# Three edits in one kernel: where subtractions run, when four blocks are split, and how the last step's results are laid out and stored

## The chip, the cores and the metric

One core of one Trainium2 chip runs the whole program. The metric is the device time of one execution in microseconds (us). Three runs of the kernel before give the times shown below.

## The reference, cut to what matters

```python
# attention with keys and values pooled by 8 over the sequence: B=8, H=8, S=576, D=64
k_p = k.reshape(B, H, Sp, 8, D).mean(axis=3); v_p = v.reshape(B, H, Sp, 8, D).mean(axis=3)
attn = softmax(q @ k_p^T / sqrt(D)); x = (attn @ v_p) as 4608 tokens x 512
...
h = x @ w_in                       # first layer: 512 -> 2048
y = relu(h) ** 2 @ w_out           # 2048 -> 512
...
gate = sigmoid(y @ w_gate); val = y @ w_val      # second layer: 512 -> 1536, twice
out = (gate * val) @ w_out2                      # 1536 -> 512
```

## The kernel before, in words

Everything is kept with features on partitions and tokens along the free axis. A float32 number is split into a rounded part (hi) and a remainder (lo); a product is three TensorE passes over such pairs. hi is a copy on ScalarE, lo a subtraction on VectorE.

**First layer.** Nine blocks of 512 tokens. For each of 16 slices f of the hidden width: 12 matmuls into a bank `h` (line 801), relu on ScalarE (line 845), square on VectorE (line 851), hi on ScalarE (line 855), lo on VectorE (line 858), 12 matmuls into four banks `acc` (line 810). Two banks `h` and three tiles `g` are in turn; the second set of matmuls of f stands behind the first set of f + 2. Attention for later blocks runs between. The result y goes to DRAM (`y_dram`).

**Second layer.** Six blocks b of 768 tokens, and the 1536 hidden columns in three chunks c: 18 steps (c, b), with b running up, down and up again. Each step uses a seven-product scheme for 2 x 2 blocks of matrices. y is cut in quadrants B11, B12, B21, B22, and needs the differences T1 to T4; weights need S1 to S4. So the matmul operands are seven tiles for each of two halves k2, hi and lo: 14 tiles, in buffers listed in `y_tags` (eleven that the first layer's weights leave free at its end, and three of their own, `ys`). `y_prep` makes them in chunk 0: it loads y from DRAM (line 1015), forms four differences for each half on GpSimd (line 1068), hi on ScalarE (line 1047), lo on VectorE (line 1051), and stores all 14 to `ys_dram` (line 1054). In chunks 1 and 2 `y_load` loads them back (line 1095). The weights of a chunk are prepared by `w_prep` (sums on GpSimd, lines 1165 to 1177; lo on VectorE, line 1132).

A step has two groups fp of products (line 1220): 14 products each, added up on VectorE from the PSUM banks (line 1251), sigmoid on ScalarE, multiplied (line 1285). The product of gate and val is again cut in quadrants; four differences t1, t3, t2, t4 for each group run on GpSimd (line 1313), each waiting for the one before; hi and lo (lines 1301, 1305) give the seven tiles `p`. Then come the outputs (line 1350): M1, M2, M6, M5, M7, M3, M4, each for two 128-row halves a and b, added up on VectorE (line 1395). Chunks 0 and 1 store partial sums in DRAM (`o_part`); chunk 2 turns each result by 32 x 32 blocks on VectorE (line 1412) and stores `out` in rows of 128 numbers, 32 partitions to a DMA (line 1425), eight DMAs for a step.

**What sets the order.** All operations are given to a planner (`Plan`) with an engine, a duration and a rank. It plays them through in time and writes out one order for each engine: at each moment the ready operation of the lowest rank goes first. On the chip each engine follows its list strictly in order, so an operation that waits holds up all behind it. All DMAs are issued by SyncE (SP).

```python
self.op("pool", 1.0, fn, deps, t - 50)      # engine, planned time, what, after what, rank
...
(y_prep if nxt[0] == 0 else y_load)(nxt[1], t + BT, t)   # the next block, during this step
```

Of the kernel before, what the change touches and what calls it, by code (L numbers as in the profile page):

```python
# [134 lines left out]
def kernel(  # L135
# [12 lines left out]
    nc = tc.nc  # L148
# [818 lines left out]

    ORDER = ("M1", "M2", "M6", "M5", "M7", "M3", "M4")
    YO = ("B11", "B21", "T2", "T1", "T3", "B22", "T4")
    W = {"M1": ("A11", "B11", "X"), "M2": ("A12", "B21", "Y"), "M6": ("S2", "T2", "X"), "M5": ("S1", "T1", "Y"),  # L970
# [29 lines left out]

    def y_prep(b, rank, at):
        t0 = b * TN
        blks = {x for x in range(t0 // NA, -(-(t0 + TN) // NA))}
        y_deps = [o for x in blks for o in y_stored[x]] + [opened]
        for name in YO:
            ys_ready[name] = []
        for k2 in range(2):
            y_prep_half(b, rank, at, k2, t0, y_deps)

    def y_prep_half(b, rank, at, k2, t0, y_deps):  # L1010
        st = {}
# [29 lines left out]
        def split(name):  # L1041
            n = YO.index(name)
            x = y_tags[2 * n + k2]

# [13 lines left out]
            o = los[name] = op("dve", 0.6, lo, [o], r)  # L1058
            ys_ready[name].append(o)
            ys_stored[b, 2 * n + k2] = op("dma", 1.3, keep, [o], r + 30, lag=2.0)  # L1060

        made = {}

        def make(name, a, c, deps):
            def fn():
                if name == "T1":
                    st["yt"] = bp["r"].tile([128, HN], F32, tag="yt", name="yt", bufs=1)
                nc.gpsimd.tensor_tensor(out=q(name), in0=q(a), in1=q(c), op=ALU.subtract)

            made[name] = op("pool", 1.0, fn, deps, rank - 30 + 0.05 * k2, take=("yt",) if name == "T1" else ())  # L1070

# [133 lines left out]
    def products(c, b, fp, t):  # L1205
# [105 lines left out]
        def diff(dst, a, z, deps):  # L1311
            def fn():
                nc.gpsimd.tensor_tensor(  # L1313
                    out=st["gate", dst], in0=st["gate", a], in1=st["gate", z], op=ALU.subtract)

            return op("pool", 1.0, fn, deps, t - 50)

# [15 lines left out]
    def outputs(c, b, t):  # L1333
# [3 lines left out]
        o_tag = {0: "o", 1: ("o", "yf", "w2s")[c]}  # L1337
        t0 = b * TN

        def mm(a, m, k2, n, deps, take):  # L1340
# [3 lines left out]
            def fn():  # L1344
# [4 lines left out]
                for j, (wa, yc) in enumerate(PASSES):  # L1349
# [4 lines left out]

            o = op("pe", 3 * DP, fn, list(deps) + [wslot_ready[c, NFP, i], p_ready[y, k2]], t + D1 * n + 0.5 * D1 * k2,
                   take=(bank[z, a],) if take else ())
# [35 lines left out]
        def add(a, key, z, deps, give=()):  # L1392
            def fn():
                x = st[a, key]
                nc.vector.tensor_tensor(out=x, in0=x, in1=st[z, a][:, 0:HN], op=ALU.add)  # L1395

            return op("dve", 0.56, fn, deps, t - 50, give=give)

        def finish(a, key, o, n):
            tt = t + D1 * n  # L1400
            if not fin:
# [4 lines left out]
                return  # L1406
            u, h = a + 2 * (int(key[0]) - 1), int(key[1]) - 1

            def turn():
# [7 lines left out]
            if first:  # L1417
                t_own[h] = ("yf", P.last["yf"])
            turned[h].append(x)
            if len(turned[h]) < 4:  # L1420
                return
            r0 = t0 + h * HN

# [9 lines left out]
        C = {}  # L1433
        order = ["M1a", "M1b", "M2a", "M2b", "M6a", "M6b", "M5a", "M5b", "M7a", "M7b", "M3a", "M4a", "M4b", "M3b"]
        for n, x in enumerate(order):
# [29 lines left out]
    for fp in range(NFP):  # L1465
        w_prep(0, fp, tl + 4 + 14 * fp, tl)
    w_prep(0, NFP, tl + 34, tl)
    y_prep(0, TB, tl)
    for step, (c, b) in enumerate(steps):
        t = TB + BT * step  # L1470
        y_users.clear()
        p_users = defaultdict(list)
# [12 lines left out]
        elif nxt:  # L1485
            (y_prep if nxt[0] == 0 else y_load)(nxt[1], t + BT, t)

# [34 lines left out]
```

## Time and profile before

| what | value |
|---|---|
| median of three runs | 1732.56 us (1730.58 to 1734.37) |
| the profiled execution's own time | 1728.68 us |
| its span, first to last instruction | 1726.6 us |
| TensorE busy | 1697.7 us, 98% |
| VectorE busy | 1184.6 us, 69% |
| ScalarE busy | 800.8 us, 46% |
| GpSimd busy | 282.4 us, 16% |
| DMA, share of 16 engines' span | 47.7% |

The busy time of an engine is the sum of its instructions' durations. TensorE's matmuls overlap, so its share counts pauses of more than about 0.2 us only. The profiled execution lies 0.22% under the median of the runs.

### The profile page before, as it was taken

Reading aid. Unit: us, or ns where it says so; the run is one execution under the profiler, and the core shown is the slowest. Engines: PE = TensorE matmul, PEld = TensorE weight load, DVE = VectorE, ACT = ScalarE, POOL = GpSimd, SP = SyncE. Lnnn points to the kernel's source line nnn. Section 1 sums busy time; section 2 is a strip of 40 time slices with the busy share of each in tenths; the row PEclk is TensorE's granted clock in tenths of the full one; section 3 lists DMA queues with packets and bytes.
Section 4 is the critical chain, followed back from the end, with each engine's and each line's share of the span. In section 5 each row is a group of like instructions: output and inputs, shape, how many; then the busy total and the mean of one; then the engine's idle time right before and its main releaser. Section 6 shows DMA issues by size and latency. Waiting matters only on the chain.

```text
span 1726.6 us, 25822 instructions
## 1 busy us (share of the span) xinstructions
PE 1697.7 (98%) x9096; PEld 1513.5 (88%) x9096; DVE 1184.6 (69%) x2200; ACT 800.8 (46%) x1927; POOL 282.4 (16%) x270
## 2 busy tenths in 40 slices
PE   8999999999999999999999999999999999999997
PEld 5778878878888888878888999999999999999997
DVE  7898668878685865423458666778655568766665
ACT  6776644444443443322446555566333345333332
POOL 0000000000000000000224334445222215222222
PEclk9999999999999999999999999999999999999999
DMA  9732344455444433020226455535555563766662
GB/s 285 250 93 75 85 124 106 122 149 126 133 113 124 106 104 95 25 87 1 73 102 225 165 201 192 195 141 171 185 195 195 197 201 114 219 201 202 201 201 38
DMA packets 224162, 251.16 MB, mean 145 GB/s; under 512 B 75040, under 2 KB 165920, under 8 KB 224032
## 3 DMA queue, kind: packets, MB, share of 16 engines
q1 hardware_dynamic: 224032, 249.50, 47.7%
q8 instruction: 72, 1.18, 0.3%
q14 instruction: 58, 0.48, 0.1%
HBM read 158.86 MB, written 82.31 MB: 140 GB/s over the span
## 4 chain that ended last, share of the span: by engine, by line
PE 91%; DVE 5%; DMA 2%; issue 1%; SPq 1%; ACT 0%; POOL 0%; DVEq 0%; POOLq 0%
PE h L801 23%; PE acc L810 22%; PE h L1220 15%; PE acc L1350 13%; PE att L1220 11%; DVE p L1305 2%; PE att L459 2%; PE att L556 2%; DVE res L1251 1%; DVE out L1051 1%; DVE res L1285 1%; DMA o<-o_part 0%; SPq L529 0%; DMA rows_q<-in_q_dram 0%; DMA o_part<-o 0%
## 5 line engine op out<-in xcount | busy, mean ns | idle before, releaser
L810 PE MATMUL acc<-g,out 128*128 128x512 f32 x1728 | 422.5, 393 | 0.0
L801 PE MATMUL h<-x,in 128*128 128x512 f32 x1728 | 420.9, 392 | 1.2 <-ACT x L792 0.7
L810 PEld LDWEIGHTS acc<-g,out 128*128 128x128 f32 x1728 | 320.9, 188 | 72.0 <-issue 4.7
L801 PEld LDWEIGHTS h<-x,in 128*128 128x128 f32 x1728 | 321.4, 188 | 71.0 <-issue 2.6
L1313 POOL TENSOR_TENSOR res<-res 128x384 f32<-128x384 f32 x144 | 166.6, 1157 | 445.6 <-ACT res L1242 316.6
L845 ACT ACTIVATE r<-h 128x512 f32<-128x512 f32 x144 | 85.9, 597 | 273.5 <-PE h L801 264.6
L1301 ACT ACTIVATE p<-res 128x384 fp32r<-128x384 f32 x252 | 131.9, 523 | 158.3 <-POOL res L1313 91.0
L1305 DVE TENSOR_TENSOR p<-res,p 128x384 fp32r<-128x384 f32 x252 | 179.2, 722 | 17.0 <-ACT p L1301 13.5
L851 DVE TENSOR_TENSOR r<-r,h 128x512 f32<-128x512 f32 x112 | 76.7, 685 | 156.7 <-ACT r L845 156.6
L1350 PE MATMUL acc<-p,in 128*128 128x384 f32 x864 | 163.4, 340 | 4.0 <-DVE p L1305 3.4
L1165 POOL TENSOR_TENSOR w2s<-w2s 128x256 f32<-128x256 f32 x18 | 15.2, 842 | 884.1 <-ACT r L845 751.3
L1350 PEld LDWEIGHTS acc<-p,in 128*128 128x128 f32 x864 | 151.1, 190 | 9.3 <-DVE p L1305 5.8
L1395 DVE TENSOR_TENSOR o<-o,acc 128x384 f32<-128x384 f32 x204 | 108.6, 546 | 47.6 <-PE acc L1350 25.2
L1242 ACT ACTIVATE res<-h 128x384 f32<-128x384 f32 x144 | 70.0, 486 | 147.5 <-PE h L1220 146.6
L858 DVE TENSOR_TENSOR g<-r,g 128x512 fp32r<-128x512 f32 x144 | 99.0, 688 | 48.8 <-ACT g L855 48.2
L1251 DVE TENSOR_TENSOR res<-res,att 128x384 f32<-128x384 f32 x144 | 79.1, 551 | 74.8 <-PE att L1220 72.9
L855 ACT ACTIVATE g<-r 128x512 fp32r<-128x512 f32 x144 | 91.2, 633 | 72.6 <-DVE r L851 65.6
L1350 PE MATMUL acc<-p,out 128*128 128x384 f32 x648 | 119.9, 335 | 0.9 <-DVE o L1395 0.9
L1350 PEld LDWEIGHTS acc<-p,out 128*128 128x128 f32 x648 | 112.8, 188 | 1.7 <-DVE o L1395 1.6
L489 ACT ACTIVATE e<-att,m 128x72 f32<-128x72 f32 x272 | 83.1, 321 | 43.1 <-DVE m L481 41.5
L1281 ACT ACTIVATE res<-res 128x384 f32<-128x384 f32 x108 | 56.6, 524 | 66.7 <-DVE res L1251 66.7
L1251 DVE TENSOR_TENSOR res<-res,h 128x384 f32<-128x384 f32 x72 | 39.6, 551 | 54.8 <-PE h L1220 54.2
(136 smaller groups left out, 2597.3 us busy)
## 6 DMA issues: line engine op xcount, KB each, us to landing
out<-ys_dram SPq DMA_DIRECT2D x60, 384.0 KB
in<-ys_dram SPq DMA_DIRECT2D x50, 384.0 KB
o_part<-o SPq DMA_DIRECT2D x96, 192.0 KB
o<-o_part SPq DMA_DIRECT2D x96, 192.0 KB
ys_dram<-out SPq DMA_DIRECT2D x36, 384.0 KB
ys_dram<-in SPq DMA_DIRECT2D x30, 384.0 KB
ys<-ys_dram SPq DMA_DIRECT2D x30, 384.0 KB
y_dram<-y SPq DMA_DIRECT2D x36, 256.0 KB
```

The costliest lines, as they stand in the source:

```text
L801: nc.tensor.matmul(out=h[:, 0:n], lhsT=w[:, a, kk * 128:(kk + 1) * 128], rhs=xs[kk][:, c], start=(kk == 0 and i == 0), stop=(kk == KT - 1 ...
L810: nc.tensor.matmul(out=y_ps[m][:, 0:NA], lhsT=w[:, a, m * 128:(m + 1) * 128], rhs=g_t[f][:, c], start=(f == f0 and i == 0), stop=(f == f1 ...
L845: nc.scalar.activation(out=r, in_=st["h"][:, 0:NA], func=ACTF.Relu)
L855: nc.scalar.activation(out=g[:, 0], in_=st["r"], func=ACTF.Copy)
L858: nc.vector.tensor_tensor(out=g_t[f][:, 1], in0=st["r"], in1=g_t[f][:, 0].bitcast(F32), op=ALU.subtract)
L1220: nc.tensor.matmul(out=st[which, z][:, 0:HN], lhsT=w[:, wa, col:col + 128], rhs=ys[y, k2][:, yc], start=(m in ("M1", "M2", "M5") and k2 == ...
L1251: nc.vector.tensor_tensor(out=r, in0=r, in1=st[which, z][:, 0:HN], op=ALU.add)
L1301: nc.scalar.activation(out=x[:, 0], in_=st["gate", key], func=ACTF.Copy)
L1305: nc.vector.tensor_tensor(out=x[:, 1], in0=st["gate", key], in1=f32(x[:, 0]), op=ALU.subtract)
L1313: nc.gpsimd.tensor_tensor(out=st["gate", dst], in0=st["gate", a], in1=st["gate", z], op=ALU.subtract)
L1350: nc.tensor.matmul(out=st[z, a][:, 0:HN], lhsT=w[:, wa, col:col + 128], rhs=p_t[y, k2][:, yc], start=(m in ("M1", "M2", "M5") and k2 == 0 ...
L1395: nc.vector.tensor_tensor(out=x, in0=x, in1=st[z, a][:, 0:HN], op=ALU.add)
```

## The change

1. The four differences of y (line 1068) and those of the second layer's products (line 1313) move from GpSimd to VectorE; the planner is given 0.57 for each in place of 1.0. GpSimd keeps the weights' sums.
2. `y_prep` for blocks 1 to 4 runs during the end of the first layer, with only the three `ys` tiles in turn: each tile is stored to `ys_dram` as soon as it is split, and the next user of the tile waits for that store. In chunk 0 the steps before blocks 1 to 4 then load the tiles (`y_load`). Block 0 and block 5 are prepared as before.
3. In the last step alone: results are turned on TensorE (three transposes of 128 x 128 for each half of a quadrant), copied out of PSUM by ScalarE, and stored by quadrant as soon as both halves are there, in 12 DMAs of 128 tokens with pieces of 64 numbers (256 bytes). The output order ends M3a, M3b, M4a, M4b; the first four outputs go by k2 first; adds get a lower rank. An identity matrix is made on GpSimd one step earlier.

```diff
@@ y_prep
-    def y_prep(b, rank, at):
+    def y_prep(b, rank, at, stage=False):
...
-            x = y_tags[2 * n + k2]
+            if stage:
+                x = y_tags[-3 + len(staged) % 3]
+                staged.append(name)
+            else:
+                x = y_tags[2 * n + k2]
...
-            ys_ready[name].append(o)
-            ys_stored[b, 2 * n + k2] = op("dma", 1.3, keep, [o], r + 30, lag=2.0)
+            ys_stored[b, 2 * n + k2] = d = op("dma", 1.3, keep, [o], r if stage else r + 30, lag=2.0)
+            if stage:
+                user[x] = [d]
+            else:
+                ys_ready[name].append(o)
...
-                nc.gpsimd.tensor_tensor(out=q(name), in0=q(a), in1=q(c), op=ALU.subtract)
-
-            made[name] = op("pool", 1.0, fn, deps, rank - 30 + 0.05 * k2, take=("yt",) if name == "T1" else ())
+                nc.vector.tensor_tensor(out=q(name), in0=q(a), in1=q(c), op=ALU.subtract)
+
+            made[name] = op("dve", 0.57, fn, deps, rank - 30 + 0.05 * k2, take=("yt",) if name == "T1" else ())
@@ products
         def diff(dst, a, z, deps):
             def fn():
-                nc.gpsimd.tensor_tensor(
+                nc.vector.tensor_tensor(
                     out=st["gate", dst], in0=st["gate", a], in1=st["gate", z], op=ALU.subtract)
 
-            return op("pool", 1.0, fn, deps, t - 50)
+            return op("dve", 0.57, fn, deps, t - 50)
@@ outputs
+        end = steps[-1] == (c, b)
...
+            r = t + 0.5 * D1 * (n + 4 * k2) if end and n < 4 else t + D1 * n + 0.5 * D1 * k2
...
-            return op("dve", 0.56, fn, deps, t - 50, give=give)
+            return op("dve", 0.56, fn, deps, t - (65 if end else 50), give=give)
+
+        def finish_end(a, key, o, u, h, tt):
+            s2 = {}
+            i2 = u // 2
+
+            def turn():
+                s2["p"] = p = ps(*END[a])
+                for j in range(HN // 128):
+                    nc.tensor.transpose(p[:, 128 * j:128 * j + 128], st[a, key][:, 128 * j:128 * j + 128], st_end["ident"])
+
+            def place():
+                if ("T", h) not in st:
+                    st["T", h] = bp["r"].tile([128, 2, HN // 128, 4, 2, 32], F32, tag="yf", name="oT", bufs=2)
+                nc.scalar.activation(
+                    out=st["T", h][:, i2, :, :, a, :],
+                    in_=s2["p"][:, 0:HN].rearrange("p (j g n) -> p j g n", g=4, n=32), func=ACTF.Copy)
+
+            def store(j):
+                r0 = t0 + h * HN + 128 * j
+                nc.sync.dma_start(
+                    out=out[r0:r0 + 128].rearrange("t (g f) -> t g f", g=4)[:, :, 64 * i2:64 * i2 + 64],
+                    in_=st["T", h][:, i2, j].rearrange("t g a n -> t g (a n)"))
+
+            o = op("pe", 0.35, turn, [o, identity], tt, take=(END[a][0],), give=(o_own[a, key],))
+            o = op("act", 0.5, place, [o], tt - 40, take=("yf",) if not turned[h] else (), give=(END[a][0],))
+            turned[h].append(o)
+            if a == 1:
+                for j in range(HN // 128):
+                    op("dma", 0.3, lambda j=j: store(j), turned[h][-2:], tt, lag=2.0)
...
-        order = ["M1a", "M1b", "M2a", "M2b", "M6a", "M6b", "M5a", "M5b", "M7a", "M7b", "M3a", "M4a", "M4b", "M3b"]
+        order = ["M1a", "M1b", "M2a", "M2b", "M6a", "M6b", "M5a", "M5b", "M7a", "M7b"]
+        order += ["M3a", "M3b", "M4a", "M4b"] if end else ["M3a", "M4a", "M4b", "M3b"]
@@ the loop over steps
+    STAGED = range(1, NB2 - 1)
...
+    for b in STAGED:
+        y_prep(b, TB - 40 + 0.5 * b, tl, True)
     y_prep(0, TB, tl)
+    END = (("h", 2), ("att", 2))
...
-            (y_prep if nxt[0] == 0 else y_load)(nxt[1], t + BT, t)
+            (y_load if nxt[0] or nxt[1] in STAGED else y_prep)(nxt[1], t + BT, t)
```

Three places show how the order moves. The lines of the changed file are shifted: 851 and 858 stay; 1132 becomes 1142, 1051 becomes 1058, 1068 becomes 1078, 1251, 1285, 1305, 1313 become 1261, 1295, 1315, 1323, 1350 becomes 1361, 1395 becomes 1407; 1418 is the new transpose.

VectorE late in the first layer's last block, before (`in_` and `out_` are tiles of the second layer's weights):

```order
L1132 TENSOR_TENSOR out_7771<-w2s,out_7771 128x512
L851 TENSOR_TENSOR r<-r,h 128x512
L1132 TENSOR_TENSOR in_7794<-w2s,in_7794 128x512
L858 TENSOR_TENSOR g<-r,g 128x512
L1132 TENSOR_TENSOR out_7814<-w2s,out_7814 128x512
```

VectorE there now (`ys_` are the three tiles in turn, `yt` and `yf` hold y and its differences):

```order
L851 TENSOR_TENSOR r<-r,h 128x512
L1078 TENSOR_TENSOR yt<-yf 128x384
L1058 TENSOR_TENSOR ys_7877<-yf,ys_7877 128x384
L858 TENSOR_TENSOR g<-r,g 128x512
L1078 TENSOR_TENSOR yf<-yf 128x384
L1058 TENSOR_TENSOR ys_7904<-yf,ys_7904 128x384
L1078 TENSOR_TENSOR yf<-yf,yt 128x384
L1142 TENSOR_TENSOR in_7912<-w2s,in_7912 128x512
```

Between the square (line 851) and the remainder (line 858) of one slice, and between two slices, there now stand operations on y: 56 splits and 32 differences within 21 slices.

VectorE in the second layer, at the end of a group of products, before:

```order
L1285 TENSOR_TENSOR res<-res 128x384
L1305 TENSOR_TENSOR p<-res,p 128x384 x4
L1251 TENSOR_TENSOR res<-res,h 128x384 x2
```

And now, at the same place:

```order
L1295 TENSOR_TENSOR res<-res 128x384
L1323 TENSOR_TENSOR res<-res 128x384 x2
L1261 TENSOR_TENSOR res<-res,att 128x384
L1315 TENSOR_TENSOR p<-res,p 128x384
L1323 TENSOR_TENSOR res<-res 128x384
L1315 TENSOR_TENSOR p<-res,p 128x384 x3
```

The four differences (line 1323) stand in VectorE's own queue, between the adds and the splits that use them.

TensorE at the very end, before (`acc_16348` and `acc_16357` are the banks of M1, M6, M7, M4, `acc_16376` is one of M2, M5, M3):

```order
L1350 MATMUL acc_16348<-p,out_13894 128x384 x3
L1350 MATMUL acc_16348<-p,out_13973 128x384 x3
L1350 MATMUL acc_16376<-p,out_14085 128x384 x3
L1350 MATMUL acc_16357<-p,out_13894 128x384 x3
L1350 MATMUL acc_16357<-p,out_13973 128x384 x3
```

And now, from the last half of M7 on:

```order
L1361 MATMUL acc_16470<-p,in_14201 128x384 x3
L1418 MATMUL h<-ident,o 128x128 x3
L1361 MATMUL acc_16480<-p,out_14212 128x384 x3
L1418 MATMUL att<-ident,o 128x128 x3
L1361 MATMUL acc_16465<-p,out_14029 128x384 x3
L1361 MATMUL acc_16465<-p,out_14129 128x384 x3
...
L1361 MATMUL acc_16470<-p,out_14029 128x384 x3
L1361 MATMUL acc_16470<-p,out_14129 128x384 x3
L1418 MATMUL h<-ident,o 128x128 x3
```

The last step has eight turns of three transposes: two stand earlier among the outputs, four between the last matmul of M7 and the last of M4, and two behind all matmuls.

## Rows read from the trace of the kernel before

**Rows 1.** Timeline of TensorE: first outputs of steps 0, 1, 4, 5, 12, 17.
```profile
939.36 2.24 PE L1350 MATMUL acc<-p,in 128*128 128x384 f32 x12
988.39 2.24 PE L1350 MATMUL acc<-p,in 128*128 128x384 f32 x12
1123.75 2.24 PE L1350 MATMUL acc<-p,in 128*128 128x384 f32 x12
1168.96 2.24 PE L1350 MATMUL acc<-p,in 128*128 128x384 f32 x12
1480.41 2.24 PE L1350 MATMUL acc<-p,in 128*128 128x384 f32 x12
1699.47 2.24 PE L1350 MATMUL acc<-p,in 128*128 128x384 f32 x12
```

**Rows 2.** Timeline of TensorE, step 0: idle time and releaser in brackets.
```profile
936.07 2.38 PE L1220 MATMUL h<-ys,in 128*128 128x384 f32 x12 [0.76 <-DVE res L1251]
950.02 6.85 PE L1350 MATMUL acc<-p,in 128*128 128x384 f32 x29 [3.04 <-DVE p L1305]
```

**Rows 3.** Timelines of VectorE and GpSimd, 936 to 951 us.
```profile
936.88 0.55 DVE L1051 TENSOR_TENSOR out<-yf,out 128x384 fp32r<-128x384 f32 x1
941.88 5.12 POOL L1313 TENSOR_TENSOR res<-res 128x384 f32<-128x384 f32 x4 [1.90 <-DVE res L1285]
944.77 1.37 DVE L1051 TENSOR_TENSOR ys<-yt,ys 128x384 fp32r<-128x384 f32 x1
```

**Rows 4.** Groups by line: busy us and mean ns, then idle before and releasers.
```profile
L1305 DVE TENSOR_TENSOR p<-res,p 128x384 fp32r<-128x384 f32 x252 | 179.2, 722 | 17.0 <-ACT p L1301 13.5
L1313 POOL TENSOR_TENSOR res<-res 128x384 f32<-128x384 f32 x144 | 166.6, 1157 | 445.6 <-ACT res L1242 316.6 <-DVE res L1285 120.6
L1301 ACT ACTIVATE p<-res 128x384 fp32r<-128x384 f32 x252 | 131.9, 523 | 158.3 <-POOL res L1313 91.0 <-DVE res L1285 66.9
```

**Rows 5.** Windows: us, then busy (count) of PE, PEld, DVE, ACT, POOL, clock, DMA.
```profile
770.00:903.00 133.00, 133.00 (x588) 110.12 (x588) 59.07 (x87) 48.97 (x83) 19.47 (x23) 1.00 0.16 54
1524.20:1568.00 43.80, 43.80 (x254) 43.80 (x253) 30.15 (x56) 16.37 (x35) 8.97 (x8) 1.00 0.68 201
```

**Rows 6.** Timeline of the first layer's last block, one slice.
```profile
852.54 0.69 DVE L851 TENSOR_TENSOR r<-r,h 128x512 f32<-128x512 f32 x1 [2.05 <-ACT r L845]
853.92 0.69 DVE L858 TENSOR_TENSOR g<-r,g 128x512 fp32r<-128x512 f32 x1 [0.70 <-ACT g L855]
859.81 2.88 PE L801 MATMUL h<-x,in 128*128 128x512 f32 x12
862.53 2.88 PE L810 MATMUL acc<-g,out 128*128 128x512 f32 x12
```

**Rows 7.** One store of a split tile: its issue; GB/s in 40 slices of 885:905.
```profile
888.55 0.32 SPq L1054 DMA_DIRECT2D ys_dram<-out  x1
GB/s 168 0 0 0 0 0 0 0 117 399 393 393 406 393 393 387 246 33 0 319 399 80 6 0 0 0 0 0 0 0 332 399 55 0 0 0 0 0 0 0
```

**Rows 8.** Timeline of the last stage: TensorE, VectorE, SyncE's queue.
```profile
1710.92 3.29 PE L1350 MATMUL acc<-p,out 128*128 128x384 f32 x18
1713.72 1.08 DVE L1395 TENSOR_TENSOR o<-o,acc 128x384 f32<-128x384 f32 x2 [0.50 <-PE acc L1350]
1715.77 7.04 SPq L1425 DMA_DIRECT2D out_dram<-oT  x8
```

**Rows 9.** DMA in 1716 to 1726 us: GB/s in 40 slices.
```profile
GB/s 0 0 74 184 168 180 174 176 174 174 174 185 182 178 164 182 178 168 176 133 174 275 281 236 203 178 176 193 195 184 180 174 178 172 176 164 121 8 0 0
```

**Rows 10.** TensorE transposes and a ScalarE copy out of PSUM: busy us, mean ns.
```profile
L537 PE MATMUL att<-ident,e 128*72 128x128 f32 x32 | 4.5, 272 | 0.0
L537 PEld LDWEIGHTS att<-ident,e 128*72 128x72 f32 x32 | 3.5, 114 | 0.9
L1242 ACT ACTIVATE res<-h 128x384 f32<-128x384 f32 x144 | 70.0, 486 | 147.5 <-PE h L1220 146.6
```

**Rows 11.** Loads of q in 128-byte pieces: GB/s in 40 slices of 102:104.
```profile
GB/s 51 95 136 195 182 144 103 46 179 13 0 0 0 0 26 67 67 95 49 10 13 3 0 3 51 82 128 184 187 141 113 72 226 371 205 410 287 410 246 451
```

More of the change, by code (lines that the diff above doesn't have):

```diff
@@ L999 @@
     ys, ys_ready, ys_stored = {}, {}, {}
-    def y_prep(b, rank, at):
+    staged = []
+    def y_prep(b, rank, at, stage=False):
         t0 = b * TN
@@ L1007, in y_prep, with y_prep_half @@
         for k2 in range(2):
-            y_prep_half(b, rank, at, k2, t0, y_deps)
-    def y_prep_half(b, rank, at, k2, t0, y_deps):
+            y_prep_half(b, rank, at, k2, t0, y_deps, stage)
+    def y_prep_half(b, rank, at, k2, t0, y_deps, stage):
         st = {}
@@ L1353, in fn @@
                         stop=(m in ("M4", "M2", "M3") and k2 == 1 and j == 2), skip_group_check=True)
-            o = op("pe", 3 * DP, fn, list(deps) + [wslot_ready[c, NFP, i], p_ready[y, k2]], t + D1 * n + 0.5 * D1 * k2,
+            r = t + 0.5 * D1 * (n + 4 * k2) if end and n < 4 else t + D1 * n + 0.5 * D1 * k2
+            o = op("pe", 3 * DP, fn, list(deps) + [wslot_ready[c, NFP, i], p_ready[y, k2]], r,
                    take=(bank[z, a],) if take else ())
@@ L1407, in finish @@
             u, h = a + 2 * (int(key[0]) - 1), int(key[1]) - 1
+            if end:
+                finish_end(a, key, o, u, h, tt)
+                return
             def turn():
@@ L1419, in finish @@
             turned[h].append(x)
+            r0 = t0 + h * HN
             if len(turned[h]) < 4:
                 return
-            r0 = t0 + h * HN
             def store(g):
@@ L1467, with make_ident @@
     w_prep(0, NFP, tl + 34, tl)
+    for b in STAGED:
+        y_prep(b, TB - 40 + 0.5 * b, tl, True)
     y_prep(0, TB, tl)
+    END = (("h", 2), ("att", 2))
+    st_end = {}
+    def make_ident():
+        st_end["ident"] = t = bp["r"].tile([128, HN], F32, tag="yt", name="ident", bufs=1)[:, 0:128]
+        make_identity(nc, t)
     for step, (c, b) in enumerate(steps):
         t = TB + BT * step
+        if step + 1 == len(steps):
+            identity = op("pool", 1.5, make_ident, [opened2], t, at=t - BT, take=("yt",))
         y_users.clear()
```

## The prediction

> **What bounds the kernel now.** I read the page's shares first: TensorE is busy 98% of 1726.6 us, so only two things can be won: pauses of TensorE, and time in which it has nothing left to do. The second layer has 18 equal steps, so the timeline of TensorE, read at the same place of each step, tells what a step loses. The reader is to see in [rows 1] that steps 12 to 17 take (1699.47 - 1480.41) / 5 = 43.81 us each, and that the early ones take longer: step 0 to 1 49.03 (5.22 over), the three from 1 to 4 together 135.36 (3.93 over), 4 to 5 45.21 (1.40 over), the seven from 5 to 12 311.45 (4.78 over). With the pause of 0.76 before the first output [rows 2] that is 16.1 us lost, most of it in steps 0 to 4, the ones that prepare y.
>
> Why they lose it is read in step 0. TensorE waits 3.04 us for a split of p on VectorE [rows 2]. Just before, GpSimd runs its four differences in 5.12 us, and a split of y on VectorE takes 1.37 us while GpSimd works, and 0.55 when it doesn't [rows 3]. Over the whole kernel a split of p takes 0.722 on the mean and a difference on GpSimd 1.157 [rows 4]. So GpSimd is slow itself, and slows the engine that the outputs wait for. VectorE is no bound by its sum: 30.15 of 43.8 us in a late step [rows 5].
>
> The end is a second place. The last matmul ends at 1710.92 + 3.29 = 1714.21 (call it L), the last add at 1714.80, and all eight stores are issued from 1715.77 on [rows 8]. Their bytes run from about 1716.5 to 1725.25 at some 176 GB/s without a gap [rows 9], and the span ends 1.35 us later. From L to the last byte it is 11.04 us, bound by the DMA.
>
> **The change, part by part.**
>
> *Differences on VectorE, in step 0.* Four differences cost 4 x 0.55 = 2.2 us instead of 5.12, so the last one is 2.9 us earlier, and no split beside them is stretched. The splits of y(1), 14 in all, leave the stretch too; two stretched ones alone take 2.7. Together that is more than the pause of 3.04. The rest of the 5.22 is what follows a pause and small waits of the same kind. Bounds: 3.0 (the pause alone) and 5.98 (5.22 + 0.76). I take 5.6, near the upper end, as both causes named by the rows go.
>
> *Steps 1 to 4.* y(2) to y(4) are only loaded. Bounds: nothing, and 3.93. The steps 5 to 12, which have loads or weights but no splits of y, lose 4.78 / 7 = 0.7 a step, with stores and loads of partial sums that steps 1 to 4 haven't both. I take 0.3 left in each, so 3.0 won. The 14 loads of a step wait in SP's queue for the tile that TensorE gives back, and behind them stand the stores of partial sums; nothing waits for those within a step, and the late steps have the same queue and lose nothing.
>
> *Step 4 to 5.* y(5) is still made there, though without GpSimd: half of 1.40, 0.7 (bounds 0 and 1.4).
>
> *Steps 5 to 12.* GpSimd stays on the weights' sums, and the partial sums are loaded as before. I take 1.0 of 4.78 (bounds 0 and 2.5, about half).
>
> *VectorE's load.* Eight differences a step add 8 x 0.55 = 4.4 us: at most 34.6 of 43.8. Hidden under TensorE's 43.8 us; if that cover went, at a step's end, it would be the second rival.
>
> *Staging in the first layer.* Four blocks of 14 splits and 8 differences add (56 + 32) x 0.55 = 48.4 us to VectorE's 59.07 of 133 [rows 5]: 81%. ScalarE gets 56 x 0.52 = 29 more on 49. What hides it: a remainder g ends at 853.92 + 0.69 = 854.61, and TensorE comes to it at 862.53; the square ends at 853.23 and its bank is needed at 859.81 [rows 6]. That is 7.9 and 6.6 us of cover in a period of 2 x 2.72 = 5.44. I take 0 here; the bound is 3 us, if VectorE is stretched by the weights' sums (19.47 us of GpSimd, up to 0.8 us more for each split beside them) and block 0's own y comes late by that.
>
> *The end.* Before L six turns of three transposes are added. Transposes follow each other at the pace of their weight loads, 0.114 [rows 10]: 6 x 3 x 0.114 = 2.05 us, on TensorE's path. After L: add, to L + 0.6; turn, 2 x 0.114 + 0.27 = 0.5; copy 0.49 [rows 10]; with hand-overs of 0.1 the store is issued at L + 1.9, and its bytes start 0.75 later, as 1715.77 to 1716.5 shows: L + 2.6. But the quadrants' stores queue. "22" is turned after the first half of M3b, with 0.52 + 1.04 + 1.04 us of matmuls and some turns still to come; its bytes start near L - 1.3, those of "12" near L + 0.4. A quadrant is 393,216 bytes in pieces of 256 bytes, a size whose store the trace does not show. Nearest rows: 512-byte stores at 176 GB/s [rows 9], which is 46.5 ns a piece on each of 16 engines, and 128-byte loads at 184 to 187 GB/s [rows 11], 11 ns a piece. Bounds by count: 11 and 46.5 ns. Both rows move about the same bytes a second, so I take 176 GB/s, 23.3 ns a piece, 2.23 us a quadrant. Then "22" ends at L + 0.9, "12" at L + 3.2, "21" at L + 5.4. Won: 11.04 - 5.4 - 2.05 = 3.6. With 11 ns SP's three issues bind, L + 4.2, won 4.8; with 46.5 ns a quadrant takes 4.46, the last byte is at L + 12.1, lost 3.1.
>
> **Sum.** 5.6 + 3.0 + 0.7 + 1.0 + 3.6 = 13.9 us. The profiled execution, 1728.68 us, becomes 1714.8; it lies 3.9 under the median of the runs, and the same difference on the median gives 1732.56 - 13.9 = 1718.7. I forecast the median.
>
> **The rivals.**
>
> *Small pieces cost by count.* The last stores run at 46.5 ns a piece: the end loses 3.1 instead of winning 3.6, and the time is 1725.4. For it: the 128-byte row is a load, not a store. Against: a piece of it is far cheaper, 11 ns [rows 11]. [...] The trace has no store of such pieces.
>
> *VectorE's own queue becomes the wait.* The differences now stand between adds and splits of one engine, and at a step's end all serve the same outputs. Then half of the second layer's 10.3 us is not won: 1723.8. For it: 34.6 of 43.8 us leaves little room at a step's end. Against: ScalarE waited 91.0 us for GpSimd's differences [rows 4], and the chain of four is 2.9 us shorter.
>
> *The three staging tiles hold up the first layer: slower.* ScalarE's copy into a tile waits for the store three splits earlier, and relu stands behind it. A store issued at 888.55 ends its bytes at about 890.5 [rows 7], so a tile's round is 0.52 (a copy, as in [rows 4]) + 0.55 + 2.0 and some 0.5 of hand-overs, 3.6 us. 56 splits in 21 slices of 5.44 us leave 6.1 us for a round. Beyond that each of 18.7 rounds pushes TensorE, less 6.6 us of cover: at 7.2 us a round 18.7 x 1.1 - 6.6 = 14 us eat the whole gain, and at 8 us the time is 1747. It decides from 7.2 on; stores would have to take 5.6 us instead of 2.0.
>
> *The gain is there, but TensorE doesn't take it* (transfers hide it): against it are the named releasers, VectorE in both of [rows 2]. I give it the chance of no change.
>
> **How the numbers follow.** Forecast 0.55, small pieces 0.17, VectorE's queue 0.15, no change 0.06, staging slower 0.07. The first three are faster by more than 0.2%, 3.5 us, which is about what a measurement of this kernel can tell from no change: 0.86 with rounding, 0.07 and 0.07. The likeliest case alone reaches from 1713 (all bounds of the second layer near their upper end) to 1722. To leave out no more than 2 in 10 the range takes in the two weaker gains and some spread of the runs: 1712 to 1728.
>
> **What would show it.** Right: step 0 to 1 within 0.5 us of 43.81, steps 1 to 4 within 0.3 each; no split of p over 0.6 us outside the steps with weights' sums; from the last matmul to the last byte 5 to 6 us, at 170 to 190 GB/s. Wrong: TensorE pauses with releasers ScalarE or VectorE before 903 us; splits or differences on VectorE named before outputs in late steps; the last stores at half the rate, or with more than 12 us behind the last matmul. The forecast fails mostly on the 256-byte price and on whether step 0 keeps a pause.

## The result and the profile after

The changed kernel takes 1711.28 us (median of 4 runs, 1710.03 to 1719.77), the kernel before 1731.57 (4 runs beside it, 1730.54 to 1734.37): ratio 0.9891, 95% interval 0.9856 to 0.9925. It is faster, by 20.3 us on the medians. The forecast was 1718.7 with a range from 1712 to 1728, so the measured time lies 0.7 us below the low end of the range. By the ratio, which compares with the runs beside it, the 1732.56 us that the forecast started from become 1713.7.

The profiled execution of the changed kernel is the longest of its four (1719.77 us, span 1718.0): TensorE's granted clock was 0.50 from 31.7 to 48.8 us, in the attention at the start, where nothing is changed, and so all later stages are shifted by about 10 us.

Windows of the profile after (us; busy time and count of PE, PEld, DVE, ACT, POOL; granted clock; DMA share; GB/s); the third answers to [rows 5]:

```profile
30.00:40.00 10.00, 10.00 (x119) 8.06 (x116) 8.60 (x24) 6.19 (x16) 0.00 (x0) 0.59 1.06 254
40.00:50.00 10.00, 10.00 (x27) 3.37 (x25) 4.98 (x10) 6.30 (x11) 0.00 (x0) 0.56 1.06 378
780.00:913.00 133.00, 133.00 (x589) 110.12 (x588) 101.33 (x173) 71.01 (x137) 18.70 (x20) 1.00 0.75 265
```

The granted clock is 0.59 and 0.56 in the first two; TensorE was busy before it fell, 8.65 of 10 us in 20:30, at 1.00. The profile of before has 1.00 in both. So the two profiles are compared stage by stage, each from its own beginning.

Timeline of TensorE after: first outputs of steps 0, 1, 4, 5, 12 and 17, to be held against [rows 1]:

```profile
948.11 2.24 PE L1361 MATMUL acc<-p,in 128*128 128x384 f32 x12
991.92 2.24 PE L1361 MATMUL acc<-p,in 128*128 128x384 f32 x12
1123.69 2.24 PE L1361 MATMUL acc<-p,in 128*128 128x384 f32 x12
1167.85 2.24 PE L1361 MATMUL acc<-p,in 128*128 128x384 f32 x12
1475.23 2.24 PE L1361 MATMUL acc<-p,in 128*128 128x384 f32 x12
1694.30 1.20 PE L1361 MATMUL acc<-p,in 128*128 128x384 f32 x6
```

Step 0 to 1 takes 43.81 us, the pitch of the late steps. Steps 1 to 4 are 0.34 over, 4 to 5 0.35, 5 to 12 0.71. The pauses of [rows 2] are gone: the view of waits names none of TensorE between 903 us and the last transpose. What is left are four short pauses that cost some 0.35 us each, three of them in steps with weights' sums.

Groups after (busy us, mean ns, idle before), which answer to [rows 4]; the difference of the products now stands under DVE:

```profile
L1315 DVE TENSOR_TENSOR p<-res,p 128x384 fp32r<-128x384 f32 x252 | 140.3, 565 | 24.7 <-ACT p L1311 19.9
L1311 ACT ACTIVATE p<-res 128x384 fp32r<-128x384 f32 x252 | 129.9, 522 | 122.8 <-DVE res L1295 74.6 <-DVE res L1323 46.6
L1323 DVE TENSOR_TENSOR res<-res 128x384 f32<-128x384 f32 x144 | 82.7, 574 | 1.4
```

A split of p takes 565 ns where it took 722, and a difference 574 where it took 1157 on GpSimd.

The first layer after: ScalarE's waits for the stores of the staging tiles in 770:913, the longest of them, and the square and the remainder g of VectorE behind it with the matmuls that need them (answer to [rows 6]):

```profile
ACT ys L1054 <- DMA ys_dram<-ys: 14.2, 12, 3.3
...
823.48 0.53 ACT L1054 ACTIVATE ys<-yt 128x384 fp32r<-128x384 f32 x1 [3.29 <-DMA ys_dram<-ys]
...
826.98 0.68 DVE L851 TENSOR_TENSOR r<-r,h 128x512 f32<-128x512 f32 x1
828.51 0.69 DVE L858 TENSOR_TENSOR g<-r,g 128x512 fp32r<-128x512 f32 x1
...
831.61 2.88 PE L801 MATMUL h<-x,in 128*128 128x512 f32 x12
834.33 1.98 PE L810 MATMUL acc<-g,out 128*128 128x512 f32 x8
```

Twelve copies waited for a store, 14.2 us together. The square ends at 827.66 and its bank is needed at 831.61; the remainder ends at 829.20 and is read at 834.33. So at least 3.95 and 5.13 us of cover are left in this stretch where [rows 6] have 6.6 and 7.9, and TensorE does not wait. From the first matmul of the second block to the first product of the second layer it is 761.37 us; before it was 761.20, and without staging (e5_no_staging) it is 761.60. So staging costs the first layer nothing that shows.

The last stage after: TensorE's last matmuls and last turn, the last copy, SyncE's stores, and GB/s in 40 slices of 1708:1718 (answers to [rows 8, 9]):

```profile
1709.76 1.29 PE L1361 MATMUL acc<-p,out 128*128 128x384 f32 x6
...
1711.79 0.52 PE L1418 MATMUL att<-ident,o 128*128 128x128 f32 x3 [0.41 <-DVE o L1407]
...
1712.35 0.49 ACT L1423 ACTIVATE oT<-att 128x384 f32<-128x384 f32 x1 [0.44 <-PE att L1418]
...
1701.41 13.61 SPq L1429 DMA_DIRECT2D out_dram<-oT  x12
...
GB/s 0 0 0 0 0 0 0 51 216 211 159 217 183 170 215 156 202 216 126 220 208 129 220 208 151 218 184 175 215 145 67 224 216 50 0 0 0 0 0 0
```

The last matmul ends at 1711.05 (L), the last byte lands near 1716.4: L + 5.3, where the kernel before had L + 11.04. Three quadrants, 1.18 MB, run without a gap from 1709.9 to 1716.3: 1.18 / 6.4 = 184 GB/s.

### The profile page after: what moved, and what is told of

It is laid out like the page before. It is cut to its first block, busy times and chain, and to the rows that moved or that the text cites. A ratio compares the mean times of both kernels' runs of the same rounds, so it can differ in the third digit from the quotient of the medians.

```text
span 1718.0 us, 25853 instructions
## 1 busy us (share of the span) xinstructions
PE 1701.8 (99%) x9120; PEld 1521.8 (89%) x9120; DVE 1218.4 (71%) x2384; ACT 805.6 (47%) x1935; POOL 64.9 (4%) x80
## 3 DMA queue, kind: packets, MB, share of 16 engines
q8 instruction: 72, 1.18, 0.3%
## 4 chain that ended last, share of the span: by engine, by line
PE 96%; DVE 1%; DMA 1%; SPq 1%; ACT 0%; issue 0%; DVEq 0%
PE h L801 23%; PE acc L810 22%; PE h L1230 17%; PE acc L1361 15%; PE att L1230 13%; PE att L459 2%; PE att L556 2%; SPq L529 0%; DMA rows_q<-in_q_dram 0%; DMA yf<-y_dram 0%; PE acc L724 0%; DVE res L1323 0%; PE acc L556 0%; PE acc L537 0%; PE att L658 0%; DVE p L1315 0%
## 5 line engine op out<-in xcount | busy, mean ns | idle before, releaser
L1361 PE MATMUL acc<-p,in 128*128 128x384 f32 x864 | 159.7, 334 | 0.0
L1315 DVE TENSOR_TENSOR p<-res,p 128x384 fp32r<-128x384 f32 x252 | 140.3, 565 | 24.7 <-ACT p L1311 19.9
L1323 DVE TENSOR_TENSOR res<-res 128x384 f32<-128x384 f32 x144 | 82.7, 574 | 1.4
L1230 PE MATMUL att<-out,in 128*128 128x384 f32 x324 | 73.9, 336 | 0.2
```

The costliest lines, as they stand in the source:

```text
L1230: nc.tensor.matmul(out=st[which, z][:, 0:HN], lhsT=w[:, wa, col:col + 128], rhs=ys[y, k2][:, yc], start=(m in ("M1", "M2", "M5") and k2 == ...
L1315: nc.vector.tensor_tensor(out=x[:, 1], in0=st["gate", key], in1=f32(x[:, 0]), op=ALU.subtract)
L1361: nc.tensor.matmul(out=st[z, a][:, 0:HN], lhsT=w[:, wa, col:col + 128], rhs=p_t[y, k2][:, yc], start=(m in ("M1", "M2", "M5") and k2 == 0 ...
```

## The experiments

All start from the changed kernel. Four parts of it can be undone apart; each run of the first group undoes some:

```diff
 S, staging
-    STAGED = range(1, NB2 - 1)
+    STAGED = ()
 E, the new end
-        end = steps[-1] == (c, b)
+        end = False
 Y, y's differences
-                nc.vector.tensor_tensor(out=q(name), in0=q(a), in1=q(c), op=ALU.subtract)
+                nc.gpsimd.tensor_tensor(out=q(name), in0=q(a), in1=q(c), op=ALU.subtract)
 P, the products' differences
-                nc.vector.tensor_tensor(
+                nc.gpsimd.tensor_tensor(
                     out=st["gate", dst], in0=st["gate", a], in1=st["gate", z], op=ALU.subtract)
```

The planner's engine and duration go with Y and P, the identity matrix with E. The table reads every profile as [rows 1] were read. The numbers are us over the pitch of 43.81: "start" is the time from the first product to the first output of step 1, over 34.90 + 43.81 (one column, since with all differences on VectorE and no staging the planner puts the first output of step 0 8.4 us earlier, with the same sum); "last stage" is from the first output of step 17 to the end of the span. Steps 12 to 17 lose 0.02 us in every profile of the table but e7b_pool_load, where it is 0.65.

| kernel | start | 1 to 4 | 4 to 5 | 5 to 12 | last stage | ratio to before, 95% |
|---|---|---|---|---|---|---|
| before | 6.35 | 3.93 | 1.40 | 4.78 | 27.16 | 1 |
| changed | 0.00 | 0.34 | 0.34 | 0.72 | 23.67 | 0.9891 (0.9856 to 0.9925) |
| e1_p_diffs | 0.00 | 0.59 | 0.33 | 0.98 | 26.41 | 0.9915 (0.9892 to 0.9937) |
| e2_staging | 0.48 | 1.04 | 1.38 | 4.80 | 27.16 | 0.9949 (0.9931 to 0.9968) |
| e3_end | 6.22 | 3.88 | 1.43 | 6.32 | 23.48 | 0.9983 (0.9966 to 1.0001) |
| e4_all_diffs | 0.00 | 0.01 | 0.34 | 0.97 | 26.46 | 0.9892 (0.9871 to 0.9913) |
| e5_no_staging | 0.00 | 0.01 | 0.34 | 0.66 | 23.28 | 0.99 (0.9876 to 0.9924) |
| e6_y_diffs | 2.79 | 6.50 | 2.34 | 4.17 | 27.12 | 1.0 (0.9987 to 1.0013) |
| e7b_pool_load | 0.00 | 0.07 | 2.00 | 10.15 | 23.59 | one run |
| e8_rows | 0.00 | 0.01 | 0.34 | 0.37 | 23.29 | 0.9904 (0.9882 to 0.9926) |
| e9_512 | 0.00 | 0.01 | 0.34 | 0.36 | 24.87 | 0.9879 (0.9855 to 0.9903) |
| e10_simple | 0.00 | 0.01 | 0.34 | 0.89 | 23.07 | 0.9885 (0.9865 to 0.9905) |

**e1_p_diffs**: S, E and Y undone, so that only the products' differences are on VectorE.

> The kernel before with only the differences of the products on VectorE; the differences of y stay on GpSimd, every y is made in the step before, the end is as before. Measured by the pitch of first outputs over 43.81 us. Before: 5.22 (step 0 to 1), 5.33 (1 to 5), 4.78 (5 to 12). Theory A (GpSimd's differences of the products are slow and stretch VectorE's splits, and that is what outputs wait for, in all steps up to 12): 5 to 12 falls under 1.0, 0 to 1 under 2.5, 1 to 5 under 2.5; time 9 to 12 us less. Rival B (the making of y in steps 0 to 4 is what costs there, whoever forms the differences): 0 to 5 together stays over 8 of 10.55, and only what steps 5 to 12 give is won, 0 to 4 us.

1717.83 us. This edit alone takes the second layer from 16.5 us of loss to 1.9. The splits of y were still in steps 0 to 4, which lose 0.9 us in all. On the medians of the runs it is 14.9 us less, more than the 9 to 12 expected.

**e2_staging**: E, Y and P undone.

> Only the splitting of y(1) to y(4) in the first layer; all differences stay on GpSimd, the end is as before. Theory A: the pauses shrink but do not go, since four differences of 1.16 us each still stand ahead of the outputs: 0 to 5 goes from 10.55 to some 4, 5 to 12 stays at 4 to 5; time 5 to 7 us less. Rival B: 0 to 5 goes under 1.5, 5 to 12 stays; 9 us less. Both: the first layer loses nothing; if the three tiles or GpSimd's 32 more differences hold it up, it is over 1 us longer and TensorE pauses before its end.

1725.16 us. Staging alone clears most of steps 0 to 4, but leaves 4 to 5 and 5 to 12 as they were. By pitches 0 to 5 lose 2.7 us, between the two theories (4 and 1.5), and the time is 7.6 us less, with the first layer as before (761.11 us). So for steps 0 to 4 either cure is nearly enough, and the two do not add up.

**e3_end**: S, Y and P undone.

> Only the last step's turn on TensorE and the stores by quadrant. Theory A: the second layer's pitches are those of before; the last step's outputs take 2.0 us longer by six turns, and from the start of the last matmul to the end of the span it is 7.3 us in place of 12.7, so 3.4 us less in all. Rival (the end gains only because the changed kernel comes to it with VectorE free of GpSimd): under 1.5 us won.

1728.18 us. The last stage is 3.7 us shorter, the steps are as before (5 to 12 lost 6.3 here; this sum differs by 1.5 us between two executions with the same steps). That is theory A in the profile; in the runs the gain does not stand clear of noise, since the interval of the ratio reaches 1.0001.

**e4_all_diffs**: S and E undone.

> Both kinds of differences on VectorE, without splitting ahead and with the end as before. Theory A: nearly all of the second layer's gain is there without the splitting ahead: 0 to 5 under 3 of 10.55, 5 to 12 under 1.0; 11 to 14 us less. Rival B: VectorE now has y's splits and differences in steps 0 to 4 as well, and 0 to 5 stays over 6; under 9 us won.

1714.2 us. With all differences on VectorE the steps lose 1.3 us without any staging: theory A, with 18.6 us less on the medians where 11 to 14 were expected. By time this kernel, with the old end, can't be told from the changed one (0.9892 beside 0.9891): what the new end is worth shows in the last stage of the profiles only. There the old end takes 26.46 us here where it took 27.16 before.

**e5_no_staging**: S undone alone.

> The changed kernel without the staging in the first layer: blocks 1 to 5 are prepared during the steps before them, as before the change; all differences on VectorE; the new end. Theory A (what the second layer won came from the differences leaving GpSimd, and staging adds nothing to that): from the first product to the last step's first output within 1.5 us of the changed kernel's 781.1 us, time 1710 to 1714 us. Rival B (the splits of y must leave steps 0 to 4): 3 to 5 us come back in steps 0 to 4, time 1715 to 1717. In both, the end is as in the changed kernel, 16.4 us of last outputs and 7 us behind the last output.

1711.54 us, as the changed kernel: theory A. From the first product to the last step's first output it is 780.7 us, with staging 781.1. Staging adds nothing that shows once the differences have left GpSimd.

**e6_y_diffs**: S, E and P undone, so that only y's differences are on VectorE.

> The kernel before with y's eight differences a block alone moved to VectorE; the products' differences stay on GpSimd, no staging, old end. Theory A (it is the products' differences, slow on GpSimd and stretching VectorE, that cost): steps 0 to 5 keep at least 7 of their 10.5 us, steps 5 to 12 keep 4 to 6, time 1727 to 1732 us. Rival C (y's differences stood in GpSimd's queue ahead of the products' ones and made them late): steps 0 to 5 fall under 4 us, time 1723 to 1726.

1730.01 us, no gain. Steps 0 to 5 lose 11.6 us with the start, as before (11.7), only spread otherwise; theory A, and rival C falls. Timeline of VectorE in step 1, then the view of TensorE's waits in 905:1170:

```profile
1033.37 1.37 DVE L1078 TENSOR_TENSOR yt<-yf 128x384 f32<-128x384 f32 x1
1034.67 2.66 DVE L1058 TENSOR_TENSOR out<-yf,out 128x384 fp32r<-128x384 f32 x2
...
PE acc L1361 <- DVE o L1407: 7.1, 5, 1.4
```

y's difference and its splits take 1.3 to 1.4 us each beside the products' differences on GpSimd, and TensorE waits 7.1 us for adds that stand behind them in VectorE's queue.

**e7_pool_load, e7b_pool_load** (the same kernel): work on GpSimd that nothing waits for, beside the splits. The order on the other engines is unchanged.

```diff
         p_ready[name, fp] = lo_of[name] = op("dve", 0.57, lo, [o], t - 50)
+
+            def load():
+                x = f32(p_t[name, fp])
+                if not scratch:
+                    scratch.append(bp["r"].tile([128, 320], F32, tag="scr", name="scr", bufs=1))
+                nc.gpsimd.tensor_tensor(out=scratch[0], in0=x[:, 0, 0:320], in1=x[:, 0, 0:320], op=ALU.subtract)
+
+            if name in LOADED:
+                p_users[name, fp].append(op("pool", 0.0, load, [o], t + 500))
...
+    scratch = []
+    LOADED = ("B11", "B22", "B21", "T1", "T2")
```

> The changed kernel, the order of TensorE, VectorE, ScalarE and SyncE unchanged, with added work on GpSimd that nothing waits for: five subtractions of 128x320 for each group of products, begun when a hi of p is there, so beside VectorE's splits (180 more instructions, some 1.0 us each, 36 groups). Theory S (GpSimd's work costs by stretching VectorE's instructions that stand ahead of what TensorE needs): the mean of a split of p rises from 0.565 to over 0.68 us and steps 0 to 12 lose 3 us or more again, time 1713.5 to 1721. Rival L (only the late results of GpSimd cost, since the chain of four took 5 us): the steps lose at most 1 us more than in the changed kernel, even if splits are stretched, time 1710 to 1713.

Its first profile (2105.16 us) had a granted clock of 0.75 on the mean, 0.94 in 0:20 and 0.71 to 0.75 in the stretches from 20 to 200; the nine other executions took 1721.76 to 1728.13 (ratio to before 0.9966, 0.9949 to 0.9983), slower than the 1713.5 to 1721 of theory S. The same kernel again:

> The kernel with the added GpSimd work again, for a profile: the first one ran at a granted clock of 0.75 from its start to its end, before the added work began, so that its steps tell nothing; its other nine executions took 1721.8 to 1728.1 us, 11 to 17 over the changed kernel. Theory S (stretched instructions on VectorE, ahead of what TensorE needs): the splits of p rise from 0.565 to over 0.68 us on the mean, and steps 0 to 17 lose some 10 us more than in the changed kernel, spread over all steps, with VectorE as the releaser. Rival W (the added work stands in GpSimd's queue ahead of the weights' sums): the loss lies in steps 5 and 11 alone, where weights are prepared.

1722.54 us, 11.3 over the changed kernel. Groups on VectorE in 920:1720 and on GpSimd; timelines of GpSimd and VectorE near 1200 and near 1153, of VectorE in step 9; TensorE's waits in 910:1710:

```profile
L1315 DVE TENSOR_TENSOR p<-res,p 128x384 fp32r<-128x384 f32 x252 | 181.4, 732 | 17.4 <-ACT p L1311 16.3
L1325 POOL TENSOR_TENSOR scr<-p 128x320 f32<-128x320 f32 x180 | 154.5, 858 | 596.4 <-ACT p L1311 594.2 <-ACT res L1252 1.9
...
1199.35 0.82 POOL L1325 TENSOR_TENSOR scr<-p 128x320 f32<-128x320 f32 x1 [1.58 <-ACT p L1311]
...
1199.52 1.07 DVE L1315 TENSOR_TENSOR p<-res,p 128x384 fp32r<-128x384 f32 x1
1200.51 0.54 DVE L1261 TENSOR_TENSOR res<-res,att 128x384 f32<-128x384 f32 x1
...
1152.37 0.92 POOL L1187 TENSOR_TENSOR w2s<-w2s 128x256 f32<-128x256 f32 x1
1153.25 1.03 POOL L1325 TENSOR_TENSOR scr<-p 128x320 f32<-128x320 f32 x1
...
1152.63 1.08 DVE L1315 TENSOR_TENSOR p<-res,p 128x384 fp32r<-128x384 f32 x1
1153.63 0.54 DVE L1261 TENSOR_TENSOR res<-res,att 128x384 f32<-128x384 f32 x1
...
1355.51 2.52 DVE L1416 TENSOR_TENSOR o<-o,acc 128x384 f32<-128x384 f32 x5 [2.75 <-DMA o<-o_part]
...
PE att L1230 <- DVE res L1261: 3.0, 2, 1.5
PE acc L1370 <- DVE o L1416: 1.9, 5, 0.8
```

The reader is to see the split that begins beside GpSimd's work and takes 1.07 us, while the add after it, with GpSimd idle, takes 0.54. The mean split is back at 732 ns. The steps lose 12.9 us though no result of GpSimd but the weights' sums is used. The loss is not spread over all steps, as theory S had it: 0.1 us in steps 0 to 3, though the splits of steps 0 to 2 take 689 ns; 5.1 in steps 4 and 5, 4.4 in steps 10 and 11 and 2.7 in steps 6 to 9. Step 4 still prepares y(5), steps 5 and 11 weights. In steps 4, 5, 10 and 11 the trace shows stretched instructions of VectorE ahead of what TensorE waits for. In step 4 (near 1153) and step 10 there are five in a row, of some 1.08 us: one begins beside an added subtraction and four beside weights' sums, which stand right behind it in GpSimd's queue. So theory S holds with a condition: in this run stretching cost where VectorE had other work to fit in. Rival W, weights' sums that come late, does not account for the 2.0 of step 4; in steps 5 and 11 it may have a part, which was not separated. The 2.7 of steps 6 to 9 are another matter: their pauses come behind adds that waited, with VectorE idle, 2.1 to 2.75 us for the load of a partial sum (last timeline), where the longest such wait of the changed kernel is 1.2. How GpSimd's work makes these loads late was not isolated.

What stretches an instruction beside GpSimd's work the trace does not say; it shows which are stretched: the splits beside GpSimd take 1.07 us here and 1.37 for y's splits in [rows 3], where they take 0.55 alone; the add of 1153.63, with one input in a PSUM bank, takes 0.54 beside GpSimd's subtraction of 1153.25.

**e8_rows**: the last step stored in rows of 2 KB.

```diff
-                    st["T", h] = bp["r"].tile([128, 2, HN // 128, 4, 2, 32], F32, tag="yf", name="oT", bufs=2)
+                    st["T", h] = bp["r"].tile([128, HN // 128, 4, 4, 32], F32, tag="yf", name="oT", bufs=2)
...
-                    out=out[r0:r0 + 128].rearrange("t (g f) -> t g f", g=4)[:, :, 64 * i2:64 * i2 + 64],
-                    in_=st["T", h][:, i2, j].rearrange("t g a n -> t g (a n)"))
+                    out=out[r0:r0 + 128], in_=st["T", h][:, j].rearrange("t g u n -> t (g u n)"))
...
-            if a == 1:
+            if len(turned[h]) == 4:
```

> The changed kernel with the last step stored in whole rows of 2 KB instead of pieces of 256 bytes: each half of 384 tokens in three DMAs of 128 rows, so only after all four of its turns; the rest is the same. It measures what a piece of another size costs. With L the end of the last matmul, bytes of the last half start near L + 2.6 and are 786 KB. By bytes (176 GB/s whatever the piece): last byte at L + 7.1 where the changed kernel has L + 5.3, time 1.8 us longer. By pieces (some 21 ns for 256 bytes, and long pieces as fast as the stores of split tiles, near 390 GB/s): last byte at L + 4.7, time 0.6 us shorter.

**e9_512**: as e8_rows, with `g` outermost in the tile, so that the pieces are 512 bytes from 128 partitions.

```diff
-                    st["T", h] = bp["r"].tile([128, HN // 128, 4, 4, 32], F32, tag="yf", name="oT", bufs=2)
+                    st["T", h] = bp["r"].tile([128, 4, HN // 128, 4, 32], F32, tag="yf", name="oT", bufs=2)
...
-                    out=out[r0:r0 + 128], in_=st["T", h][:, j].rearrange("t g u n -> t (g u n)"))
+                    out=out[r0:r0 + 128].rearrange("t (g f) -> t g f", g=4), in_=st["T", h][:, :, j].rearrange("t g u n -> t g (u n)"))
```

> The kernel with whole rows at the end, but with the four parts of a row apart in the on-chip tile, so that each piece is 512 bytes, as in the stores of the kernel before, and comes from 128 partitions where those came from 32. If a piece of 512 bytes costs 46.5 ns as there, whatever the partitions: 176 GB/s, the last half takes 4.5 us, last byte at L + 7.1 (L + 4.8 with pieces of 2 KB), and the span is 2.3 us longer than with those. If it was the 32 partitions: 28 ns a piece or less, 290 GB/s or more, last byte at most at L + 5.5.

1713.15 and 1711.46 us, neither apart from the changed kernel. GB/s in 40 slices of 1701:1711, first with rows of 2 KB, then with 512 bytes:

```profile
GB/s 0 0 0 0 0 0 0 0 319 377 393 377 393 385 385 385 131 262 344 401 369 410 369 385 393 213 0 0 0 0 0 0 0 33 33 0 0 0 0 0
```

```profile
GB/s 0 0 0 111 285 285 303 279 276 305 283 268 303 297 275 260 317 291 268 264 317 283 283 291 291 158 0 0 0 0 0 0 0 66 0 0 0 0 0 0
```

In the first, L is 1702.68, and the bytes end near 1707.5: L + 4.8, as by pieces. But the span still ends at 1709.2, L + 6.5, as in e5_no_staging, so nothing is won. In the second, 512-byte pieces run at some 285 GB/s (16 x 512 / 285 = 28.7 ns a piece), where those of before had 46.5 ns [rows 9]; the last byte is at L + 6.4 because both halves queue, which the bound of L + 5.5 had left out. The last stage is 1.6 us longer than with rows of 2 KB (24.87 and 23.29), which the medians of the runs do not show. What differs from the stores of before is 128 partitions in place of 32, and 256 KB in place of 192 KB to a DMA; the two were not separated. The two rates are 176 beside 285 GB/s, and the stores of before came from four groups of 32 partitions in turn.

**e10_simple**: S undone, and the rows of e8_rows.

> What the runs so far point to: all differences on VectorE, no staging in the first layer, the new end with whole rows. Theory A: within 1 us of the kernel without staging at the same clock, 1709 to 1714 us, since neither part was shown to be worth more than 0.5 us. If staging and the stores by quadrant are worth something after all: 1714 to 1717.

1713.24 us (6 runs), inside theory A's range: with the changed kernel, e5_no_staging and e8_rows within one interval. No version beats the changed kernel measurably; the staging can be left out.

## Why the prediction was right, and which term was off

The direction and the places were right: TensorE's pauses in the early steps and the end. Against the profile of before the terms came out so:

| term | forecast | measured |
|---|---|---|
| step 0, with the pause before | 5.6 | 6.35 |
| steps 1 to 4 | 3.0 | 3.59 |
| step 4 to 5 | 0.7 | 1.06 |
| steps 5 to 12 | 1.0 | 4.06 |
| first layer | 0 | -0.17 |
| the end | 3.6 | 3.49 |
| sum | 13.9 | 18.38 |

Of the signs for "right" all came but one: step 2 kept 0.34 us where 0.3 were allowed.

**The term that was off** is "Steps 5 to 12", 1.0 us taken with an upper bound of 2.5. It gave the loss there to the weights' sums, which stay, and to the loads of partial sums. The runs show otherwise: with P undone the loss is 4.80 (e2_staging), 6.32 (e3_end) and 4.17 (e6_y_diffs), with P alone on VectorE it is 0.98 (e1_p_diffs). So most of it came from the products' differences, as in step 0. The row was there to read. Timelines of VectorE and GpSimd in step 5, before, and of VectorE in step 9:

```profile
1204.04 1.37 DVE L1305 TENSOR_TENSOR p<-res,p 128x384 fp32r<-128x384 f32 x1
1205.33 0.54 DVE L1251 TENSOR_TENSOR res<-res,att 128x384 f32<-128x384 f32 x1
...
1200.74 5.53 POOL L1313 TENSOR_TENSOR res<-res 128x384 f32<-128x384 f32 x4 [0.49 <-DVE res L1285]
...
1359.34 1.95 DVE L1395 TENSOR_TENSOR o<-o,acc 128x384 f32<-128x384 f32 x4 [2.60 <-DMA o<-o_part]
```

The add that frees a bank stands behind a split stretched to 1.37 us, beside four differences of 5.53: the pattern of [rows 3], 260 us later. Two pauses, in steps 6 and 9, came behind adds that waited for a load of a partial sum, as in the last row; why these too are gone with P alone was not isolated. Where GpSimd got work again (e7b_pool_load), pauses of this kind came back in steps 6 to 9. With 4.06 in that term the sum would have been 17.0 and the forecast 1715.6.

**The rest of the distance**: 18.4 us by terms stand against 20.3 on the medians. On the means of the same runs the distance is 18.9. The rest is no changed stage; it lies within what the start varies by itself: from the span's start to the second block's first matmul the profiles take from 142.13 (before) to 151.84 us (changed).

**Steps 0 to 4** were sized from both causes, slow differences and splits of y, as if each had its share. They are one mechanism: e1 removes nearly all of it alone, e2 most of it. The upper bound of 5.98 counted 0.76 for the way to the first output, which lost 1.13 (6.35 - 5.22). A part of the 5.22 that is no pause is read in windows of the profile before (columns as in the section on the result):

```profile
950.00:953.00 3.00, 2.98 (x9) 2.98 (x10) 1.75 (x4) 1.47 (x4) 1.83 (x2) 0.50 0.52 189
954.00:957.00 3.00, 3.00 (x19) 3.00 (x18) 1.05 (x3) 0.76 (x2) 2.02 (x2) 1.00 1.01 304
```

Right behind the pause of 3.04 us the granted clock is 0.50, and 9 matmuls start in 3 us where 19 do at 1.00. Ten fewer, at 3.00 / 19 us each, make some 1.6 us of the 5.22, an estimate from these counts; the prediction had it as "what follows a pause". The clock falls behind the same pause in e3_end (0.50 in 957:960), and in the changed kernel, without the pause, it is 1.00 from 913 to 1714 us.

In e7b GpSimd's work beside VectorE's cost where VectorE had enough work to be held up by it: 5.1 us in steps 4 and 5 (VectorE busy 36.44 of 44 us in 1168:1212), and 0.1 in steps 0 to 3 (27.32 in 992:1036). Which of the two ways counts more, the late results or the stretched instructions, is shown only on one side: e7b loses 12.9 us with no late results but those of the weights' sums, 9.5 of them in steps where stretched instructions stand ahead of the pauses; late results without stretching were not tried.

**The end** came out by its parts: 2.02 us more before the last matmul ends where 2.05 were worked out (2.02 / 18 = 0.112 a transpose), and the last byte as below. The 0.1 of a hand-over was the author's estimate; the last copy starts 0.04 behind its turn (1712.35, after 1711.79 + 0.52). But 0.7 of the 3.49 belong to the differences: with them on VectorE the old end takes 26.46 us (e4_all_diffs), so the new end won 2.8 there, and 3.7 on the kernel before (e3_end).

**Rival, small pieces cost by count** (46.5 ns): wrong in its price. The 256-byte pieces moved at 184 GB/s where the sum had 176, and the last byte came at L + 5.3 where L + 5.4 was worked out. The ground of that price was wrong all the same, and the hit partly luck: it took the bytes a second to be the same whatever the piece, from a store out of 32 partitions and from loads read at the peak of slices of 0.05 us, while stores from 128 partitions ran at 184 GB/s in 256-byte pieces, at 285 in 512 (e9_512) and at 385 in 2 KB (e8_rows). The rival's price of a piece, that of the 512-byte rows, was one of 32 partitions.

**Rival, VectorE's own queue**: wrong for this kernel, since no step kept more than 0.36 us; it appeared in e7b, where the instructions in that queue are stretched (a mean split of p at 732 ns, where the changed kernel has 565).

**Rival, staging tiles**: wrong in the time, but the waits came. The prediction gave a tile's round 3.6 of 6.1 us; twelve copies waited for a store, up to 3.29 us, and the cover took it, with 3.95 us left at the least. The opposite surprise is that staging, with 56 splits and 32 differences in the first layer, buys nothing (e5_no_staging).

## What to carry to other kernels

When an engine that shares work with another looks idle enough, look at the mean duration of the same instruction with and without its neighbour active: here moving 192 short instructions from GpSimd to VectorE, which is then busy 76% at the end of the first layer (101.33 of 133 us), made VectorE's other work faster than it was (a split of p 565 ns where it took 722). Where one line of the trace explains a loss in one step, look for the same line in all steps before giving their loss to something else. Two cures for one wait do not add up; undo each alone before keeping both.

## What the runs showed of the hardware

Stores from 128 partitions ran at 184 GB/s in pieces of 256 bytes (the changed kernel, 128 KB to a DMA), at 285 in 512 (e9_512) and at 385 in 2 KB (e8_rows, 256 KB to a DMA in both). For 512 bytes from 32 partitions, 192 KB to a DMA, it was 176 [rows 9]. An earlier last byte did not end the program earlier: with 2 KB rows the bytes ended at L + 4.8 where e5_no_staging has L + 5.2, and the span at L + 6.5 in both. And one of ten executions of e7_pool_load had a granted clock of 0.75 on the mean, 0.94 in its first 20 us and 0.71 to 0.75 from 20 to 200, and took 2105 us; it was there before the added work began, and nothing in the runs says why.
